# Gated linear attention followed by a bilinear feed-forward: natural feature order, prefix sums in two exact one-pass parts, v cast by the DMA, loads held behind the transposes, and a relaid program

## The chip, the cores and the metric

One core of one Trainium2 chip. The metric is the device time of one execution in microseconds (us). The kernel before was tuned already: 224.56 us, median of 3 runs (224.02 to 224.88). A profile is one traced execution; its span is about 2 us shorter than the time of the same run (222.4 against 224.5).

PE is TensorE (PEld its weight loads), DVE is VectorE, ACT is ScalarE, POOL is GpSimd, SP is SyncE. L207 is line 207 of that kernel's own file, so one piece of code has different line numbers in different kernels.

## The reference, cut to what matters

```python
# q, k, v, alpha: (4 batches, 8 heads, 768 steps, 48); 3072 tokens, d_model 384, d_ff 1536
for t in range(S):
    state = alpha[:, :, t, :, None] * state + einsum('bhd,bhe->bhde', k[:, :, t], v[:, :, t])
    y[:, :, t] = einsum('bhd,bhde->bhe', q[:, :, t], state)
x = y.transpose(0, 2, 1, 3).reshape(3072, 384)      # the 8 heads' 48 features side by side
out = ((x @ w_a) * (x @ w_b)) @ w_out
```

Both kernels work on six chunks: two batches (the chunk's two "units") times 256 steps each. For a chunk, a prefix sum of log alpha gives the decays; keys and queries scaled by them are transposed; scores, a masked product ("inner") and the product with the state brought along ("carried") make `y`; and `y`, evicted to SBUF as `xT`, feeds the two feed-forward matrices. The feed-forward of one chunk covers the attention of the next.

## The kernel before

The parts that the change touches:

```python
def stA(ch, u):                                  # prefix sum: one fp32 matmul
    nc.tensor.matmul(p, lhsT=ut_f32, rhs=ch.l2[:, u]..., start=True, stop=True)
...
def stS(ch, u):                                  # carried state
    for p in range(P2):
        for g in range(2):
            for r in range(2):                   # two row tiles, one PSUM bank (g)
                nc.tensor.matmul(y[rs, g, p, :], lhsT=state, rhs=queriesT(ch, u, p, g, rs), ...)
...
def stG(ch, u, eng):                             # 16 features of each head pair's block of 64 + 64 rows
    for t in range(KT):                          # come from the fourth pair's block, evicted first:
        for g in range(2):                       # six "gap" matmuls per unit, then a second eviction
            nc.tensor.matmul(ch.y[u][:, g, t, :], lhsT=gap[:, t]..., rhs=ch.xT[:, KT, 2 * g + u, :], ...)
    evac(ch, u, 0, KT, eng)
```

The heads lie in blocks of 64 rows of which 48 are used. So that the feed-forward contracts over three full tiles of 128 rows, the fourth block is moved into the free rows of the other three by matmuls, and the weight rows are loaded in that odd order (`load_ab`, 24 DMAs). All loads are fp32; chunk 2's keys and queries are transposed on TensorE, those of chunks 3 to 5 by a DMA transpose; loads go out as soon as their buffers are free. The order of work is a table (`START`, `PLAN`) of operations attached to feed-forward steps, and PSUM banks come from a rotating pool.

Of the kernel before, what the change touches and what calls it, by code (L numbers as in the profile page):

```python
# [9 lines left out]
BF16 = mybir.dt.bfloat16  # L10
AF = mybir.ActivationFunctionType
# [3 lines left out]
START = [  # L15
    (0, "new"), (0, "ln"), (0, "ld a 0 Y"), (0, "ld a 1 Y"), (0, "ld k 0 Y"), (0, "L 0 V"), (0, "ld q 0 Y"), (0, "warm 18"), (0, "ld v 0 Y"),
    (0, "ld k 1 Y"), (0, "ld q 1 Y"), (1, "new"), (0, "ld v 1 Y"), (0, "L 1 P"), (0, "A 0"), (0, "gate_w q 1"), (0, "W 0 512"), (0, "W 512 1024"),
    (1, "ld a * P"), (0, "W 1024 1536"), (0, "Wo 4 8"), (0, "Wo 0 4"), (0, "A 1"), (1, "ld v 0 P"), (0, "Wo 8 12"), (1, "ld k 0 P"),
    (1, "ld q 0 P"), (1, "ld q 1 P"), (0, "warm 24"), (1, "ld k 1 P"), (1, "ld v 1 P"), (0, "mk 0 V"), (0, "dec P"), (0, "v 0 S"), (0, "mq 0 V"),
    (0, "C 0 0 V"), (0, "warm 6"), (0, "C 0 1 S"), (0, "D 0 0 s2"), (0, "K 0 P y2"), (0, "warm 8"), (0, "warm 14"), (0, "v 1 S"), (0, "S 0"),  # L20
    (0, "mk 1 V"), (0, "D 0 1 s2"), (0, "mq 1 V"), (0, "warm 18"), (0, "Y 0 V"), (0, "C 1 0 V"), (0, "G 0 V"), (0, "D 1 0 s2"), (0, "C 1 1 S"),
    (0, "K 1 V y2"), (0, "ff 1 0"), (0, "ff 0 0"), (0, "S 1"), (0, "D 1 1 s2"), (0, "Y 1 S"), (0, "ff 3 0"), (0, "G 1 S"), (0, "ff 2 0"),
    (0, "ff 1 1"), (0, "ff 2 1"), (0, "ff 0 1"), (0, "ff 3 1"),
]



PLAN = {
    0: [(9, 1, "L * V"), (14, 1, "A 1"), (16, 1, "A 0"), (16, 1, "dec P"), (16, 2, "new"), (16, 2, "ld a * P"), (22, 2, "ld v * P"),
        (24, 1, "v 0 S"), (25, 1, "mk 0 V"), (25, 2, "ld k * P"), (25, 2, "ld q * P"), (25, 1, "mq 0 V"), (25, 1, "C 0 0 V"), (25, 1, "C 0 1 S"),  # L30
        (25, 1, "D 0 0 s2"), (25, 1, "K 0 P y2"), (26, 1, "mk 1 V"), (26, 1, "S 0"), (26, 1, "mq 1 V"), (26, 1, "D 0 1 s2"), (27, 1, "Y 0 S"),
        (27, 1, "v 1 S"), (27, 1, "C 1 0 V"), (27, 1, "C 1 1 V"), (27, 1, "G 0 S"), (27, 1, "D 1 0 s2"), (27, 1, "K 1 V y2"), (27, 1, "S 1"),
        (27, 1, "D 1 1 s2"), (27, 1, "ff 1 0"), (27, 1, "ff 3 0"), (27, 1, "Y 1 S"), (27, 1, "G 1 S"), (27, 1, "ff 0 0"), (27, 1, "ff 2 0")],
    1: [(0, 1, "ff 1 1"), (2, 3, "new"), (5, 1, "ff 3 1"), (5, 3, "ld k * P"), (5, 3, "ld a * P"), (6, 1, "ff 2 1"), (6, 2, "L * V"),
        (7, 3, "ld q * P"), (10, 1, "ff 0 1"), (10, 2, "A 0"), (10, 2, "A 1"), (11, 2, "mk 0 V"), (12, 2, "dec P"), (12, 3, "ld v * P"),
        (12, 2, "mq 0 V"), (13, 2, "mk 1 V"), (13, 2, "mq 1 V"), (14, 2, "C 0 0 V"), (14, 2, "v * S"), (15, 2, "C 0 1 S"), (15, 2, "C 1 0 V"),
        (15, 3, "L * P"), (16, 2, "D 0 0 s2"), (16, 2, "K * P"), (17, 2, "C 1 1 S"), (18, 2, "S 0"), (18, 4, "new"), (18, 2, "D 0 1 s2"),
        (19, 4, "ld q * P"), (19, 4, "ld k * P"), (20, 2, "D 1 0 s2"), (20, 2, "Y 0 S"), (20, 3, "A 0"), (20, 4, "ld v * P"), (21, 2, "G 0 V"),
        (21, 3, "mk 0 V"), (22, 3, "A 1"), (22, 2, "S 1"), (22, 2, "D 1 1 s2"), (23, 3, "mk 1 V"), (24, 2, "Y 1 S"), (25, 2, "G 1 S"),
        (25, 3, "mq 0 V"), (25, 3, "T 0 Y"), (26, 3, "mq 1 V"), (27, 3, "dec D"), (27, 3, "T 1 Y"), (27, 4, "ld a * P")],  # L40
    2: [(6, 3, "v * P"), (6, 3, "D 0 0 s2"), (8, 4, "L * P"), (9, 3, "K * V"), (10, 3, "S 0"), (10, 3, "D 0 1 s2"), (12, 5, "new"), (12, 3, "Y 0 S"),
        (13, 3, "D 1 0 s2"), (13, 3, "G 0 S"), (14, 4, "A 1"), (15, 3, "S 1"), (15, 3, "D 1 1 s2"), (16, 4, "A 0"), (16, 3, "Y 1 S"),
        (16, 4, "mk 0 V"), (19, 4, "mq 0 V"), (19, 4, "T 0 Y"), (20, 3, "G 1 S"), (22, 4, "mk 1 V"), (23, 4, "mq 1 V"), (24, 4, "v * S"),
        (24, 4, "dec D")],
    3: [(0, 4, "K * V"), (5, 5, "ld a * P"), (6, 5, "ld q * P"), (6, 4, "S 0"), (6, 4, "D 0 0 s2"), (7, 5, "ld v * P"), (7, 4, "D 0 1 s2"),
        (7, 5, "L * V"), (8, 4, "T 1 Y"), (9, 5, "ld k * P"), (11, 4, "D 1 0 s2"), (11, 4, "Y 0 S"), (12, 4, "G 0 S"), (12, 5, "A 0"),
        (13, 4, "S 1"), (13, 4, "D 1 1 s2"), (14, 5, "mk 0 V"), (14, 5, "A 1"), (15, 5, "mq 0 V"), (16, 4, "Y 1 V"), (16, 5, "dec D"),
        (19, 5, "mk 1 V"), (19, 4, "G 1 S"), (20, 5, "mq 1 V"), (20, 5, "T 1 Y"), (20, 5, "T 0 Y"), (26, 5, "v * V")],
    4: [(0, 5, "K * V"), (1, 5, "D 0 0 s2"), (6, 5, "D 1 0 s2"), (6, 5, "S 0"), (9, 5, "D 0 1 s2"), (12, 5, "Y 0 V"), (13, 5, "G 0 V"),
        (14, 5, "S 1"), (14, 5, "D 1 1 s2"), (17, 5, "Y 1 S"), (23, 5, "G 1 S")],  # L50
    5: [],
}
# [3 lines left out]
def kernel(  # L56
# [23 lines left out]
    G = DP - D  # L80
    HC = C // 2
    NT = B * C

# [5 lines left out]
    ps = ctx.enter_context(tc.tile_pool(name="ps", bufs=1, space=bass.MemoryType.PSUM))  # L89


    one = cst.tile([C, 1], F32, name="one")
    nc.vector.memset(one, 1.0)
    ident = cst.tile([C, C], BF16, name="ident")
    make_identity(nc, ident)

    ut_f32 = cst.tile([C, C], F32, name="ut_f32")
    make_upper_triangular(nc, ut_f32, val=1.0, diag=True)
    nc.vector.memset(ut_f32[0:HC, HC:C], 0.0)

    mask = cst.tile([C, 2, 2, HC], BF16, name="mask")
    mtmp = cst.tile([C, 2, 2, HC], BF16, name="mtmp")
    for t, first in ((mask, 0), (mtmp, -HC)):
        nc.gpsimd.memset(t, 0.0)
        nc.gpsimd.affine_select(out=t, in_=t, compare_op=ALU.is_gt, fill=1.0, base=first,
                                pattern=[[0, 2], [0, 2], [-1, HC]], channel_multiplier=1)
        nc.gpsimd.memset(t[:, 1, 0, :], 0.0)
        nc.gpsimd.affine_select(out=t[:, 1, 0, :], in_=t[:, 1, 0, :], compare_op=ALU.is_gt, fill=1.0, base=first + 1,
                                pattern=[[-1, HC]], channel_multiplier=1)

# [3 lines left out]

    S0 = [cst.tile([C, B, P2, DP], BF16, name=f"S0{i}") for i in range(2)]
    Sm = [cst.tile([C, 2, P2, DP], BF16, name=f"Sm{i}") for i in range(2)]
    Qp, Kp, QKp, bls = [], [], [], []
    for i in range(2):
        t = cst.tile([C, 2, 2, 2, H, DP], BF16, name=f"QKp{i}")
        (nc.gpsimd if i else nc.vector).memset(t[:, :, :, :, :, D:].rearrange("p b j r h d -> p (b j r h) d"), 0.0)  # L120
        QKp.append(t)
        Qp.append(t[:, :, 0])
        Kp.append(t[:, :, 1])
        t = cst.tile([C, B, P2], F32, name=f"bl{i}")
        (nc.gpsimd if i else nc.vector).memset(t, 0.0)
        bls.append(t)

    gap = cst.tile([C, KT, 2, DP], BF16, name="gap")
    nc.vector.memset(gap, 0.0)
    for t in range(KT):  # L130
        nc.vector.tensor_copy(gap[:, t, :, D:], ident.rearrange("p (r d) -> p r d", r=2)[:, :, t * G:(t + 1) * G])
    for i in range(2):
        for t in (S0[i], Sm[i]):
            (nc.gpsimd if i else nc.vector).memset(t, 0.0)
    nc.vector.tensor_copy(mask[HC:C], mtmp[HC:C])

    wa_t = cst.tile([128, KT, d_ff], BF16, name="wa_t")
    wb_t = cst.tile([128, KT, d_ff], BF16, name="wb_t")
    wo_t = cst.tile([128, NFF, d_model], BF16, name="wo_t")

    def load_ab(lo, hi):
        fs = slice(lo, hi)
        for w, t in ((moe_w_a, wa_t), (moe_w_b, wb_t)):
            two = w[:KT * 2 * D, fs].rearrange("(t r d) f -> r d t f", r=2, d=D)
            rest = w[KT * 2 * D:, fs].rearrange("(r t g) f -> r g t f", r=2, g=G)
            for r in range(2):
                nc.gpsimd.dma_start(out=t[r * DP:r * DP + D, :, fs], in_=two[r])
                nc.gpsimd.dma_start(out=t[r * DP + D:(r + 1) * DP, :, fs], in_=rest[r])

    def load_o(lo, hi):  # L150
        nc.gpsimd.dma_start(out=wo_t[:, lo:hi, :], in_=moe_w_out[lo * 128:hi * 128, :].rearrange("(k p) f -> p k f", p=128))



    class Chunk:
        def __init__(ch, c):
            ch.c = c
            ch.s, ch.b0 = c // 2, c % 2 * 2
            ch.kqT, ch.m, ch.y = {}, {}, {}

    chunks = [Chunk(c) for c in range(NCH)]
    ALL = slice(0, 2)
    ONE = (slice(0, 1), slice(1, 2))

# [321 lines left out]
```

## Time and profile before

| | before |
|---|---|
| span of the profile | 222.4 us |
| TensorE busy | 199.5 us (90%) |
| TensorE busy in 0-20, 20-40, 40-120, 120-218 us | 14.5, 17.9, 71.5, 95.6 us |
| warm-up matmuls | 88, 7.7 us |
| gap matmuls | 72, 6.0 us |

The prediction below shows the page. Here is the table of stretches in the four pieces that the accounting uses. The columns are the bounds, the length, busy time of PE, PEld, DVE, ACT and POOL, the granted clock, the DMA share and GB/s:

```profile
0.00:20.00 20.00, 14.47 (x290) 11.93 (x291) 13.03 (x24) 9.20 (x16) 13.14 (x34) 1.00 1.01 191
20.00:40.00 20.00, 17.94 (x281) 12.20 (x282) 12.80 (x23) 11.52 (x23) 16.16 (x24) 1.00 1.08 188
40.00:120.00 80.00, 71.48 (x1061) 43.36 (x1069) 55.54 (x75) 41.72 (x80) 26.44 (x23) 0.98 0.82 201
120.00:218.00 98.00, 95.58 (x931) 51.04 (x945) 50.64 (x69) 43.08 (x78) 0.00 (x0) 1.00 0.34 68
```

The length less the second figure is TensorE's idle time: 5.5, 2.1, 8.5 and 2.4 us. The clock of 0.98 in the third row is one spell at half clock, from 59.7 to 63.1 us.

In the list of waits a row has the engine, its line, what released it, then us in total, times, and the longest:

```profile
PE f L207 <- DVE l L187: 3.6, 1, 3.6
PE y L292 <- DVE Sm L343: 2.1, 1, 2.1
PE y L308 <- DVE m L282: 1.6, 2, 1.4
```

The first wait is the start; the others are attention that was hurried through with no feed-forward left to cover it. No DMA is in the list, though the DMA row is full for the first 72 us.

### The profile page before, as it was taken

Reading aid. Unit: us, or ns where it says so; the run is one execution under the profiler, and the core shown is the slowest. Engines: PE = TensorE matmul, PEld = TensorE weight load, DVE = VectorE, ACT = ScalarE, POOL = GpSimd, SP = SyncE. Lnnn points to the kernel's source line nnn. Section 1 sums busy time; section 2 is a strip of 40 time slices with the busy share of each in tenths; the row PEclk is TensorE's granted clock in tenths of the full one; section 3 lists DMA queues with packets and bytes.
Section 4 is the critical chain, followed back from the end, with each engine's and each line's share of the span. In section 5 each row is a group of like instructions: output and inputs, shape, how many; then the busy total and the mean of one; then the engine's idle time right before and its main releaser. Section 6 shows DMA issues by size and latency. Waiting matters only on the chain.

```text
span 222.4 us, 6004 instructions
## 1 busy us (share of the span) xinstructions
PE 199.5 (90%) x2558; PEld 118.5 (53%) x2584; DVE 132.0 (59%) x189; ACT 105.9 (48%) x195; POOL 55.7 (25%) x79
## 2 busy tenths in 40 slices
PE   3798799999799969899779999899999989999991
PEld 3487665566575545464345565464555445544460
DVE  5569657458736879942887914889508763045400
ACT  3470467742346955644517654577233334254420
POOL 8358949737200048400280000000000000000000
PEclk9999999999889999999999999999999999999997
DMA  7999999999999103999879945400881000320022
GB/s 168 261 175 154 200 181 168 271 266 323 325 282 259 38 3 82 265 271 180 65 173 264 197 114 113 93 0 4 126 172 37 3 3 0 83 58 3 0 71 71
DMA packets 37874, 30.70 MB, mean 138 GB/s; under 512 B 27084, under 2 KB 34008, under 8 KB 37848
## 3 DMA queue, kind: packets, MB, share of 16 engines
q0 software_dynamic: 8480, 19.27, 37.4%
q1 hardware_dynamic: 29368, 11.05, 25.6%
q8 instruction: 20, 0.33, 0.6%
q14 instruction: 6, 0.05, 0.1%
HBM read 25.97 MB, written 4.74 MB: 138 GB/s over the span
## 4 chain that ended last, share of the span: by engine, by line
PE 75%; DVE 12%; ACT 4%; issue 3%; DMA 2%; POOL 1%; SPq 1%; POOLq 0%; DVEq 0%; ACTq 0%
PE f L379 20%; PE f L360 19%; PE f L370 18%; PE f L207 4%; DVE m L282 4%; PE y L308 3%; PE s L281 3%; PE y L292 2%; PE f L254 1%; PE y L315 1%; DVE xT L297 1%; DVE kqT L260 1%; PE f L203 1%; DMA bl<-row 1%; DVE tmp L342 1%
## 5 line engine op out<-in xcount | busy, mean ns | idle before, releaser
L360 PE MATMUL f<-xT,wa_t 128*128 128x512 bf16 (+1 forms) x229 | 59.6, 361 | 1.2 <-ACT kqT L258 0.3
L370 PE MATMUL f<-xT,wb_t 128*128 128x512 bf16 (+1 forms) x225 | 59.0, 361 | 1.1 <-issue 0.5
L379 PE MATMUL f<-wo_t,prod 128*128 128x384 bf16 x288 | 48.6, 326 | 0.7 <-DVE prod L372 0.7
L379 PEld LDWEIGHTS <-prod 128*128 128x128 bf16 x288 | 27.8, 98 | 19.7 <-DVE prod L372 1.1
L360 PEld LDWEIGHTS <-wa_t 128*128 128x128 bf16 x240 | 22.5, 99 | 21.2 <-issue 1.0
L370 PEld LDWEIGHTS <-wb_t 128*128 128x128 bf16 x240 | 22.4, 99 | 21.2 <-issue 1.3
L282 DVE TENSOR_TENSOR m<-s,mask 128x1024 bf16<-128x1024 f32 x24 | 29.3, 1222 | 4.3 <-PE s L281 4.0
L381 ACT ACTIVATE ot<-f 128x384 f32<-128x384 f32 x24 | 11.8, 490 | 35.0 <-PE f L379 34.9
L187 POOL TENSOR_TENSOR l<-la 128x768 f32<-128x768 f32 (+1 forms) x3 | 4.6, 1532 | 41.1 <-ACT la L185 22.3
L299 ACT ACTIVATE xT<-y 128x256 bf16<-128x256 f32 (+1 forms) x18 | 10.7, 596 | 8.6 <-PE y L308 5.6
L207 PE MATMUL f<-l,ut_f 128*128 128x384 f32 x24 | 11.1, 562 | 3.6 <-DVE l L187 3.6
L215 DVE TENSOR_TENSOR QKp<-k_t,invb 128x768 bf16<-128x768 f32 x12 | 12.4, 1036 | 1.0 <-ACT invb L211 1.0
L281 PE MATMUL s<-kqT 64*64 64x128 bf16 x384 | 11.5, 222 | 1.4 <-DVE kqT L260 0.7
L215 DVE TENSOR_TENSOR QKp<-q_t,beta 128x768 bf16<-128x768 f32 x12 | 11.6, 977 | 0.5 <-DMA q_t<-in_q_dram 0.5
L342 DVE TENSOR_TENSOR tmp<-s,S 128x384 f32<-128x384 f32 x4 | 2.2, 558 | 15.5 <-PE s L329 15.5
L281 PEld LDWEIGHTS <-kqT 64*64 64x64 bf16 x384 | 7.7, 106 | 6.0 <-issue 3.9
L210 ACT ACTIVATE invb<-f 128x384 f32<-128x384 f32 x12 | 5.9, 492 | 10.0 <-DVE le L208 10.0
L185 ACT ACTIVATE la<-a_t 128x1536 f32<-128x1536 f32 (+1 forms) x7 | 9.1, 1295 | 3.1 <-DMA a_t<-in_alpha_dram 3.1
L208 DVE TENSOR_TENSOR le<-f,la 128x384 f32<-128x384 f32 x12 | 6.7, 556 | 4.9 <-PE f L207 4.7
L258 ACT ACTIVATE kqT<-f 128x1024 bf16<-128x1024 bf16 x5 | 5.1, 1022 | 9.0 <-PE f L254 8.9
L292 PE MATMUL y<-kqT,S 64*64 64x128 bf16 x96 | 7.0, 221 | 2.4 <-DVE tmp L342 1.5
L308 PE MATMUL y<-m,vx 64*48 64x128 bf16 x384 | 7.7, 220 | 1.6 <-DVE m L282 1.6
(233 smaller groups left out, 280.7 us busy)
## 6 DMA issues: line engine op xcount, KB each, us to landing
out_dram<-ot SPq DMA_DIRECT2D x48, 96.0 KB, 2.2
a_t<-in_alpha_dram POOLq DMA_DIRECT2D x5, 768.0 KB, 12.5
v_t<-in_v_dram POOLq DMA_DIRECT2D x4, 768.0 KB, 13.6
k_t<-in_k_dram POOLq DMA_DIRECT2D x4, 768.0 KB, 14.0
q_t<-in_q_dram POOLq DMA_DIRECT2D x4, 768.0 KB, 13.5
wo_t<-in_moe_w_out_dram POOLq DMA_DIRECT2D x3, 384.0 KB, 6.7
wa_t<-in_moe_w_a_dram POOLq DMA_DIRECT2D x6, 144.0 KB, 4.2
wb_t<-in_moe_w_b_dram POOLq DMA_DIRECT2D x6, 144.0 KB, 4.4
```

The source lines that it names most:

```text
L185: nc.scalar.activation(out=ch.la[:, us].rearrange("p b h r d -> p (b h r d)"), in_=ch.a[:, us].rearrange("p b h r d -> p (b h r d)"), func ...
L207: nc.tensor.matmul(p, lhsT=ut_f32, rhs=ch.l2[:, u].rearrange("p h d -> p (h d)"), start=True, stop=True)
L215: eng.tensor_mul(dst[ch.c % 2][:, u, :, :, :D], src[:, u].rearrange("p h r d -> p r h d"), by[:, u])
L281: nc.tensor.matmul(s2[g * HC:(g + 1) * HC, r, p, rk, :], lhsT=keysT(ch, u, 2 * h + p, g, r, rk), rhs=queriesT(ch, u, 2 * h + p, g, rs), st ...
L282: nc.vector.tensor_mul(m.rearrange("p r a k s -> p (r a) (k s)"), s2.rearrange("p r a k s -> p (r a) (k s)"), maskn(4))
L292: nc.tensor.matmul(y[rs, g, p, :], lhsT=lhsT, rhs=queriesT(ch, u, p, g, rs), start=(p == 0), stop=False, skip_group_check=True)
L299: nc.scalar.activation(out=o_, in_=i_, func=AF.Copy)
L308: nc.tensor.matmul(ch.y[u][r * DP:r * DP + D, g, p, :], lhsT=ch.vx[g * HC:(g + 1) * HC, u, 2 * p + r, rk, :], rhs=ch.m[u, p // 2][g * HC:( ...
L360: nc.tensor.matmul(ap, lhsT=wa_t[:, kk, f * 128:(f + 1) * 128], rhs=ff_x(ch, us)[:, kk], start=(kk == 0), stop=(kk == KT - 1))
L370: nc.tensor.matmul(bp, lhsT=wb_t[:, kk, f * 128:(f + 1) * 128], rhs=ff_x(ch, us)[:, kk], start=(kk == 0), stop=(kk == KT - 1))
L379: nc.tensor.matmul(op, lhsT=ch.prod[:, f, m * C:(m + 1) * C], rhs=wo_t[:, f, :], start=(f == 0), stop=(f == NFF - 1))
L381: nc.scalar.activation(out=ot, in_=op, func=AF.Copy)
```

## The change

Intent: lay `y` out in the natural order of the 384 features, so that the gap matmuls, the second eviction and the odd weight order go; replace each fp32 prefix sum by two float32r matmuls, one of the rounded values and one of the remainders; let the DMA cast v to bf16; order the carried-state matmuls so that neighbouring row tiles go to different banks; transpose chunk 2 by DMA as well; hold the next chunk's loads behind the transposes; and write the schedule as one program of single operations with explicit banks. The diff, cut to its core:

```diff
-def stA(ch, u): ... matmul(p, lhsT=ut_f32, rhs=ch.l2[:, u])
+def high(ch, us, eng): ... lh = float32r copy of l2                 # chunks 1 to 5
+def low(ch, us, eng):  ... ll = l2 - lh
+def cum2(ch, u, i):
+    for t in (ch.lh, ch.ll):
+        nc.tensor.matmul(p, lhsT=utr, rhs=t[:, u]..., start=(t is ch.lh), stop=(t is ch.ll))
...
-def stG(ch, u, eng): ... six gap matmuls, second eviction
+PIECES = [(h, j) for h in range(H) for j in range(D * h // DP, (D * h + D - 1) // DP + 1)]
+def inner(ch, u):          # 12 pieces of 64 rows, in natural order: 48 matmuls a unit (were 32)
+    ...
+def carried(ch, u, cross): # the two row tiles r in turn, with g = 1 - r: different banks
+    for n in range(3):
+        for c in range(2):
+            for r in range(2):
+                g = 1 - r if cross else r
+                if g == 0 and ch.s == 0: continue
+                ...
...
-            setattr(ch, n, ld.tile([C, 2, H, 2, D], F32, name=n + "_t"))
+            setattr(ch, what, ld.tile([C, 2, H, 2, D], BF16 if what == "v" else F32, name=what + "_t"))
...
+def gate_t(x, u):          # POOL touches the transposed tile: its queue waits for the transpose
+    nc.gpsimd.tensor_copy(go, x.kqT[int(u)][0:1, 0, 0, 0, 0:1])
...
-START = [...]; PLAN = {...}
+PROGRAM = """
+0: c1; warm 70 0; cz 0 V; cs 0 V
+...
+0: W b 768 1536; Ce 0 1 S; mq 1 V; warm 11 1
+...
+0: k 1 1 V; as 1 0; Y 1; SA 1; b 1 0 5; X 1 S; pr 1 0; as 0 0
+...
+2: v 0 S; gatet 1; D 1 0 2
+3: ld a * P
+...
+"""
```

In the program, `a`, `b`, `as`, `pr` and `o` are the feed-forward's matmuls, copy, product and output; `Y` is inner, `SA`/`SB` carried, `X` the eviction, `W` and `ld` loads, `warm n` n warm-up matmuls of 128 columns.

## The prediction

> **What bounds the kernel now.** I read the page's busy shares first, then the slices, then the table of stretches, then the chain that ended last piece by piece, to get the price of each piece of TensorE work.
>
> ```profile
> span 222.4 us, 6004 instructions
> PE 199.5 (90%) x2558; PEld 118.5 (53%) x2584; DVE 132.0 (59%) x189; ACT 105.9 (48%) x195; POOL 55.7 (25%) x79
> PE   3798799999799969899779999899999989999991
> DMA  7999999999999103999879945400881000320022
> ...
> PE 75%; DVE 12%; ACT 4%; issue 3%; DMA 2%; POOL 1%; SPq 1%; POOLq 0%; DVEq 0%; ACTq 0%
> ```
>
> TensorE is busy 90% and is 75% of the chain, so it is the bound. The DMA row is also full for the first 13 slices (72 us): a second limit early, which at present stops TensorE almost nowhere. Where TensorE is not full, the table of stretches says (a row has its bounds, its length, then PE, PEld, DVE, ACT and POOL busy, the granted clock, DMA share and GB/s):
>
> ```profile
> 0.00:10.00 10.00, 5.09 (x25) 3.40 (x26) 5.07 (x13) 3.71 (x5) 6.67 (x21) 1.00 0.98 210
> 20.00:30.00 10.00, 8.04 (x173) 6.61 (x172) 6.90 (x13) 4.13 (x9) 7.88 (x13) 1.00 1.07 198
> 50.00:60.00 10.00, 8.38 (x190) 5.87 (x187) 8.02 (x12) 2.90 (x5) 5.65 (x5) 0.98 1.05 324
> 110.00:120.00 10.00, 7.48 (x134) 4.43 (x137) 8.33 (x10) 4.08 (x9) 6.19 (x5) 1.00 1.06 204
> 200.00:210.00 10.00, 9.95 (x47) 4.54 (x47) 5.30 (x8) 4.74 (x8) 0.00 (x0) 1.00 0.01 2
> ```
>
> The last row is the pure feed-forward end, with nothing to wait for; the others are the start and the two worst stretches of attention. TensorE's idle of 22.9 us (222.4 - 199.5) splits, row by row of that table, into about 5.5 before 20 us, 2.1 from 20 to 40, 8.5 from 40 to 120, 2.3 from 120 to 218 and 4.4 behind the last matmul. The prices, from the chain:
>
> ```profile
> 38.51 0.83 PE s L236 x64
> ...
> 126.38 7.80 PE f L379 x48
> 134.83 0.66 PE s L329 x55
> ...
> 143.42 0.65 PE f L360 x3
> ...
> 146.26 0.34 PE y L315 x6
> ...
> 147.95 0.45 PE y L292 x12
> ...
> 149.49 0.65 PE f L207 x2
> ...
> 151.43 0.56 PE y L308 x32
> 151.99 0.75 PE f L370 x3
> ```
>
> A triple of 512-column feed-forward matmuls costs 0.65, an output matmul of 384 columns 7.80/48 = 0.1625. One fp32 prefix sum (384 columns) also costs 0.65. The carried-state group costs 0.45 for 16 (a few lie among the scores), 28 ns each; inner products 0.45 for 32, 14 ns each, plus 0.1 for coming from full-array work; the next full-array triple pays another 0.1 (0.75 for 0.65). State products cost 0.66/55 = 12 ns each, decay sums 0.83 a chunk, the gap-filling matmuls 0.34 a unit, eight transposes 0.45.
>
> **What the Trainium skill says.** "FP8 and Floating Point Precision", section TensorE Precision Notes: true FP32 makes four passes through the array. The trace agrees: 0.65 is 4.0 times 0.1625 at the same 384 columns. It does not price the float32r type in passes; no run here has it yet. "TensorE: Matmul & The Clock Gate", section "Wait — 56ns, not 53.3ns?": a warm matmul starts N/2.4 GHz plus about 2.5 ns after its predecessor; 384 columns give 162.5 ns, which the trace shows exactly. "TensorEngine Tiling (Array Packing)", sections Key Properties and Gotcha 1: changing the tiling mode drains the engine, and different row tiles can't use one PSUM bank at the same time. The trace has the drain (0.1 each way), and its carried-state group, which sends neighbouring row tiles to one bank, runs at 28 ns against 14 for scores. "DMA: Bandwidth & Descriptors", section Issuing engines are not separate DMA queues: all issuers share the same 16 engines. The trace agrees: SyncE's loads alone moved 261 GB/s from 4.5 to 13.6 us at a full DMA row, so early loads on both queues compete.
>
> **The change part by part** (TensorE microseconds, counts from the two instruction orders).
> - Prefix sums: chunks 1 to 5 replace 10 fp32 sums by two passes each. 10 x (0.65 - 2 x 0.1625) = -3.2. It adds a rounding copy (ACT 0.5 to 0.85) and a subtraction (DVE 0.95 for 768 columns, 0.56 for 384) per chunk: about 4 on ACT, 5 on DVE, before the sum, in engines at 48% and 59%.
> - Natural feature order: the 72 gap matmuls go, 12 x 0.34 = -4.1. Also gone is the two-step eviction (0.38 to 0.42, gap matmuls, 0.81), now one of about 0.81: some 0.7 less latency per unit, but only where TensorE has nothing else. It costs pieces that straddle a tile: inner products 384 to 576, +192 x 14 ns = +2.7.
> - Carried state: 192 to 240 matmuls (chunks 0 and 1 skip the zero state), ordered so that the two row tiles use different banks: 192 x 28 = 5.4 to 240 x 14 = 3.4, so -2.0.
> - Chunk 2 transposes and its decay go from TensorE to DMA: 32 transposes, -1.8, and 64 decay matmuls in the trace, -0.8. Last-state products are not made for the last two chunks: 384 to 320, -0.8.
> - Passages between tiling modes: 78 to 68, at 0.1, -1.0.
> - Feed-forward: the same columns. More half-width pairs (36 where there were 16), and the before trace shows 0.33 for a half triple against 0.65, so no TensorE cost; each extra ACT or DVE half pair costs some 0.15 of fixed time.
> The sum: -3.2 - 4.1 + 2.7 - 2.0 - 2.6 - 0.8 - 1.0 = -11.0. Priced this way the old kernel has 188.5 of TensorE work (feed-forward 140.1, attention 40.6, passages 7.8), the rest being 22.9 idle, about 7.5 of warm-up matmuls and some 3.5 of cold clock and latency. The new one has 177.5.
>
> Waits. Of the 8.5 idle between 40 and 120 us, most lies where a chunk's attention was hurried through while no feed-forward was left to cover it (the chain passes through evictions and exponentials from 71 to 79 us, and through the decay's DMAs at 105 to 110 us). The new program spreads scores, masks and outputs singly among feed-forward groups, with explicit banks and half-width groups of chunk 1. I credit half of these 8.5 and some of the later 2.3: -5.
>
> The start. Key and query of the first half come before the second half's decay input, and constants are fewer, so the first half's chain should be 1 to 2 earlier. Against that stand weights: the third weight block (columns 256 to 768 of the first matrix) is queued behind v, the first weight blocks and half of chunk 1. Reads up to and with it are 6 x 0.39 + 0.39 + 0.79 + 0.39 + 1.57 + 0.79 = 6.3 MB; at the 261 GB/s of SyncE's loads from 2 us on it lands at 26 us, while the first full block of feed-forward wants it at about 21. The old kernel had matmuls of that stage only from 22.4 on and reached continuous feed-forward at 28.6. So the start is about even; I charge +1.5. The wider weight DMAs (6 in place of 24) should avoid the hole seen in DMA from 14 to 18 us (103 GB/s).
>
> Casting v on the DMA saves little: the reads are the same, ACT and DVE still copy it into the padded layout. Loads behind transposes mean less contention for the latter; that is part of the waits above. The end (4.4 behind the last matmul) is unchanged.
>
> Total: 222.4 - 11.0 - 5 + 1.5 = 208 in the profile; the timed median is 2.1 over the profiled span, so 210; because the whole program was laid out for TensorE I shade it to 209.
>
> **The rivals.**
> - Weights or loads starve TensorE. For: the DMA row is full until 72 us and the old order had its weights earlier. Against: the old kernel's list of TensorE waits names no DMA at all. It would take back 3 to 8: 212 to 217.
> - float32r does not run in one pass. At two passes each, the 3.2 vanish and ACT and DVE work is added for nothing: about 213. At four, 10 x 0.65 is added on top: near 219.
> - The waits move. In-order engines now carry a fixed interleaving; a mask product on DVE (1.22 each, 24 of them) or an activation copy queued behind another chunk's exponentials holds a bank, and TensorE waits for it. For: explicit banks remove the pool's rotation, DVE stays near 132 to 137 busy. Against: 59% busy leaves room. Then only the 11 of TensorE work is won, or less: 213 to 216.
> - It goes better: most idle between 20 and 218 us (12.9) is covered. Then 222.4 - 11 - 9 = 202, timed 204.
>
> **Range and chances.** The -11.0 is counted and I trust it to 3 either way; waits and start are worth -10 to +4 between them. That gives 202 to 217. Slower by over 2% needs starvation beyond all the gains; within 2% means above 220.1, where two rivals must meet. Faster 0.90, same 0.07, slower 0.03.
>
> **What would show it.** Right: prefix matmuls of 384 columns spaced 0.16 apart; no gap matmuls; carried-state groups of 12 in about 0.17 plus passage; inner groups of 48 in 0.67; idle TensorE from 40 to 120 us near 4 and PE busy near 190 of 207. Wrong: waits of feed-forward matmuls on a weight DMA between 21 and 40 us; prefix matmuls at 0.33 or more; carried-state groups still at 28 ns each; TensorE idle of more than 10 after 40 us, released by mask products or activation copies.

## The result, and the profile after

209.97 us, median of 4 runs (209.25 to 210.48), against 224.72 (224.02 to 225.68) for the kernel before on the same chip. The ratio is 0.9339, 95% interval 0.9294 to 0.9384. A ratio here is the mean time of one kernel's fast runs over that of the other's fast runs of the same rounds, so it isn't quite the ratio of the medians. Executions over 1.5% slower than the fastest of the same kernel are left out of the means.

The page after:

```profile
span 207.3 us, 6249 instructions
PE 192.6 (93%) x2702; PEld 121.6 (59%) x2718; DVE 139.9 (67%) x223; ACT 101.2 (49%) x192; POOL 38.0 (18%) x54
PE   8988499999999989999998899999999999999991
...
PEclk9999859999999999999999999999999999999998
DMA  6999999999310697997959919699457200004155
...
PE 53%; issue 24%; DMA 9%; DVE 6%; ACT 4%; POOL 2%; POOLq 0%; ACTq 0%; DVEq 0%
```

TensorE is the bound as before, and fuller. (The 24% of "issue" in the chain are nearly all one piece of 39.5 us, from 36.6 to 76.2 us, in which the chain follows POOL as it waits at the first gate. TensorE was busy for 38.7 of these us.) Two things are new: the 4 in its fifth slice, and the 8 and 5 in the clock row at that place and just after it. The stretches say how much:

```profile
0.00:20.00 20.00, 17.34 (x351) 15.15 (x351) 16.17 (x30) 10.17 (x17) 14.82 (x30) 1.00 1.19 222
20.00:40.00 20.00, 16.67 (x236) 12.10 (x238) 10.29 (x22) 9.88 (x23) 8.90 (x9) 0.83 1.26 222
40.00:120.00 80.00, 76.52 (x1265) 50.52 (x1269) 63.26 (x101) 44.73 (x90) 9.54 (x10) 1.00 0.82 157
120.00:204.00 84.00, 82.04 (x853) 43.80 (x862) 50.20 (x71) 36.38 (x64) 4.76 (x5) 1.00 0.46 91
```

Idle from 40 to 120 us fell from 8.5 to 3.5 us, and behind 120 from 2.4 to about 1 (the last matmul ends near 203). But from 20 to 40 us TensorE idles 3.3 us where it was 2.1, and its mean clock there is 0.83.

The pieces of the chain (start, us, what) carry the new prices, and one DMA wait:

```profile
104.13 7.59 DMA a_t<-in_alpha_dram
...
116.36 0.34 PE psum L596 x2
...
137.51 0.17 PE psum L738 x12
```

The two one-pass matmuls of one prefix sum of 384 columns cost 0.34 us (the fp32 one cost 0.65 before), and twelve carried-state matmuls cost 0.17 us, 14 ns each (28 before).

TensorE's own waits after:

```profile
PE psum L738 <- issue: 2.5, 1, 2.5
PE psum L722 <- DVE prod L802: 1.7, 1, 1.7
...
PE psum L722 <- DMA kqT<-QKp: 0.6, 1, 0.6
```

"issue" means that TensorE waited for nothing that the profile shows. That longest wait is in TensorE's timeline (start, length, engine, line, operation, shape, count, and in brackets the idle time ahead):

```profile
22.27 0.81 PE L789 MATMUL psum<-xT,wa_t 128*128 128x256 bf16 x6 [0.64 <-ACT xT L773]
23.01 0.58 PE L738 MATMUL psum<-m,vx 64*64 64x128 bf16 x25
26.07 0.85 PE L738 MATMUL psum<-m,vx 64*64 64x128 bf16 x23 [2.48 <-issue]
```

The stall falls in the middle of 48 identical inner products of one unit, all on the same operands: 25 run, nothing for 2.48 us, then the other 23. At 24.8 us, during the stall, the clock drops to 0.50 and stays there until 31.6. TensorE is busy 5.6 us of these 6.8, of which half is lost: about 2.8.

So the 15.1 us of the span (222.4 - 207.3) come from: TensorE work -11.0 (as priced; tested below), waits from 40 us on -6.4 (5.0 + 1.4), the spell at half clock of the kernel before, which is gone, -1.7; what remains, +4, is the start. Read directly the start gives a little more: warm-up matmuls 11.2 us for 7.7 (+3.5), half clock +2.8, idle before 40 us 6.0 for 7.6 (-1.6), +4.7 in all. The two readings differ by 0.7, which is the accuracy of this account. (The warm-ups fill time in which TensorE would have waited, so what they and the smaller idle time come to is best read together.)

### The profile page after: what moved, and what is told of

The parts are those of the page before. It is cut to its first block, busy times and chain, and to the rows that moved or that the text cites. A ratio compares the mean times of both kernels' runs of the same rounds, so it can differ in the third digit from the quotient of the medians.

```text
span 207.3 us, 6249 instructions
## 1 busy us (share of the span) xinstructions
PE 192.6 (93%) x2702; PEld 121.6 (59%) x2718; DVE 139.9 (67%) x223; ACT 101.2 (49%) x192; POOL 38.0 (18%) x54
## 2 busy tenths in 40 slices
DMA packets 52587, 29.42 MB, mean 142 GB/s; under 512 B 42760, under 2 KB 49672, under 8 KB 52560
## 4 chain that ended last, share of the span: by engine, by line
PE 53%; issue 24%; DMA 9%; DVE 6%; ACT 4%; POOL 2%; POOLq 0%; ACTq 0%; DVEq 0%
PE psum L789 28%; PE psum L812 15%; DMA a_t<-in_alpha_dram 7%; PE psum L738 4%; DMA kqT<-QKp 2%; ACT la L553 1%; DVE l L559 1%; PE psum L722 1%; PE psum L693 1%; ACT kqT L660 1%; PE psum L574 1%; PE psum L596 1%; DVE S L518 1%; DVE vx L513 1%; DVE m L727 1%
## 5 line engine op out<-in xcount | busy, mean ns | idle before, releaser
L789 PE MATMUL psum<-xT,wa_t 128*128 128x512 bf16 (+1 forms) x262 | 57.2, 344 | 1.3 <-ACT xT L773 0.6
L789 PE MATMUL psum<-xT,wb_t 128*128 128x512 bf16 (+1 forms) x262 | 56.4, 338 | 0.6 <-issue 0.5
L812 PE MATMUL psum<-wo_t,prod 128*128 128x384 bf16 x288 | 51.5, 326 | 0.1
L727 DVE TENSOR_TENSOR m<-psum,mask 128x1024 bf16<-128x1024 f32 x24 | 29.0, 1220 | 7.9 <-PE psum L722 7.7
L773 ACT ACTIVATE xT<-psum 128x768 bf16<-128x768 f32 x11 | 8.9, 808 | 14.4 <-PE psum L738 14.3
L553 ACT ACTIVATE la<-a_t 128x768 f32<-128x768 f32 (+1 forms) x8 | 9.3, 1165 | 11.6 <-DMA a_t<-in_alpha_dram 11.6
L738 PE MATMUL psum<-m,vx 64*64 64x128 bf16 x576 | 10.9, 221 | 2.8 <-issue 2.5
L722 PE MATMUL psum<-kqT 64*64 64x128 bf16 x384 | 10.3, 219 | 2.7 <-DVE prod L802 1.7
L570 PE MATMUL psum<-wz 128*128 128x128 bf16 x154 | 11.2, 238 | 1.0 <-DVE one L493 1.0
L570 PEld LDWEIGHTS <-wz 128*128 128x128 bf16 x154 | 10.3, 108 | 1.9 <-DVE one L493 1.0
```

What stands on the lines that cost most here:

```text
L553: nc.scalar.activation(out=ch.la[:, us].rearrange("p b h r d -> p (b h r d)"), in_=ch.a[:, us].rearrange("p b h r d -> p (b h r d)"), func ...
L570: nc.tensor.matmul(w[:, :C], lhsT=wz, rhs=wz, start=True, stop=True)
L722: nc.tensor.matmul(s2[g * HC:(g + 1) * HC, r, p, rk, :], lhsT=ch.kqT[u][rs, 1, rk, 2 * h + p, g * HC:(g + 1) * HC], rhs=queriesT(ch, u, 2 ...
L727: nc.vector.tensor_mul(m.rearrange("p r a k s -> p (r a) (k s)"), ch.s2[u, h].rearrange("p r a k s -> p (r a) (k s)"), maskn(4))
L738: nc.tensor.matmul(y[c * DP:(c + 1) * DP, g, j // 2 * C:(j // 2 + 1) * C], lhsT=lhsT, rhs=rhs, start=(g, c) not in begun, stop=False, skip ...
L773: nc.scalar.activation(out=o_, in_=i_, func=AF.Copy)
```

## The experiments

Ten kernels, in three sets on two chips; the kernel before had medians of 225.25 us in the first set and 224.99 and 224.95 in the others. Two further ideas never ran. Putting the carried-state matmuls back into the order in which neighbouring row tiles write one bank was rejected by the race check, so the 14 ns against 28 stand as read from the traces alone. And loading v as fp32 does not fit beside the rest: the work pool then wants 96 KB a partition, and 92.5 are left.

The question is why the start cost +4. Before the runs I counted the matmuls and weight loads that TensorE had begun at each stall. In the kernel after, the two stalls on "issue" near 20 and 24 us lie ahead of counts 705 and 961, 256 apart. The page lists an instruction queue of 21 packets, 0.34 MB, so 16 KB each, and TensorE's 5,420 matmuls and weight loads are 21 times 256 and a few over. The Trainium skill, "Trainium Architecture — The Big Picture", section The software stack, gives an instruction 64 bytes; then a packet is 256 of them, which agrees with the distance of the stalls. That is the theory of the instruction fetch: TensorE runs dry because the next block comes late over DMA engines that are full of loads. The rival from the prediction is weights that come late.

### wide_warm: fewer instructions ahead of the stall

```diff
-    wz = cst.tile([C, C], BF16, name="wz")
+    wz = cst.tile([C, 512], BF16, name="wz")
-        for _ in range(n):
-            nc.tensor.matmul(w[:, :C], lhsT=wz, rhs=wz, start=True, stop=True)
+        for _ in range(-(-n // 4)):
+            nc.tensor.matmul(w[:, :512], lhsT=wz[:, :C], rhs=wz, start=True, stop=True)
```

> The warm-up matmuls are 512 columns wide, a quarter as many: the same TensorE time, some 220 TensorE instructions fewer in the first 20 us. Theory (the 2.48 us stall among the second unit's inner products is a late 16 KB fetch of TensorE's own instructions, and the half clock from 24.8 to 31.6 us follows from it): no stall over 1 us in that group, no half clock before 200 us, time 3 to 5 below the changed kernel (205 to 207), unless a weight wait of up to 1.5 shows in its place. Rival (the stall is a weight or mask wait that the profile misses): the stall stays in the same group and the time stays at 210.

206.81 us (205.46 to 207.73), ratio 0.9189 [0.9139, 0.9239]: 1.6% faster than the change. The time fell as expected, but neither of the two signs came: a stall of over 1 us remained, and so did a half clock. The stall, 1.88 us, fell after another number of the same inner products:

```profile
23.49 0.36 PE L738 MATMUL psum<-m,vx 64*64 64x128 bf16 x11
25.72 1.14 PE L738 MATMUL psum<-m,vx 64*64 64x128 bf16 x37 [1.88 <-issue]
```

Its stalls now lie ahead of counts 447 and 703: again 256 apart, though the work around them is other work. The half clock lasted 3.4 us in place of 6.8.

### more_warm: more instructions ahead of it

```diff
-0: c1; warm 70 0; cz 0 V; cs 0 V
+0: c1; warm 90 0; cz 0 V; cs 0 V
```

> 20 more warm-up matmuls (40 instructions) in the first batch, before anything depends on them. Fetch theory: the gaps are tied to the count of TensorE instructions, 256 apart, so the long gap moves 40 instructions up the program: it falls after about 5 of the 48 inner products of the second unit and no longer after 25, and the short one near 20.2 us moves by as many. Rival (a data wait): the gap stays after 25 inner products. Time within 1 per cent of the changed kernel.

Forty more instructions ahead (20 matmuls and their 20 weight loads), and the stall moves forty instructions back in the work, from the 25th to the 5th inner product. That is what a boundary in the instruction stream does; a late weight or operand would stop the same matmul as before.

```profile
24.98 0.30 PE L738 MATMUL psum<-m,vx 64*64 64x128 bf16 x5
27.36 0.81 PE L738 MATMUL psum<-m,vx 64*64 64x128 bf16 x43 [2.08 <-issue]
```

The stalls lie ahead of counts 705 and 961, as in the change; the first of them grew to 1.54 us.

206.69 us in one run (its state is unknown), 1.6% below the change, where I had expected it within 1%. The stall of 2.08 us was there, but there was no half clock from 24 to 34 us (1.00 throughout), and the run was 3 us faster than the change. So most of the cost of the start seems to hang on the clock that falls after the stall, rather than on the stall; it is one run.

### fp32_sums: the prefix sums undone

```diff
-        for t in (ch.lh, ch.ll):
-            nc.tensor.matmul(p, lhsT=utr, rhs=t[:, u]..., start=(t is ch.lh), stop=(t is ch.ll))
+        cum(ch, u, i)                                # one fp32 matmul, as in chunk 0
-        "H": lambda x, u, e: high(x, us(u), ENG[e]),
-        "L": lambda x, u, e: low(x, us(u), ENG[e]),
+        "H": lambda x, u, e: None,
+        "L": lambda x, u, e: None,
```

> All prefix sums in fp32 as before, the rounding copies and subtractions dropped. Theory of the prediction: TensorE gets 10 x 0.32 = 3.2 us of work back, so 2.5 to 3.5 slower than the changed kernel (212.5 to 213.5). Rival (two passes behind a copy and a subtraction save nothing, because the chain through ACT and DVE is longer): within 1 us of the changed kernel, or faster.

212.37 us (210.49 to 213.35), ratio 0.9431 [0.9372, 0.949]; against the change's 0.9339 that is 1.0%, some 2.1 us, a little under the 2.5 to 3.5 that I expected. In the profile the span is 210.8 (+3.5) and TensorE is busy 196.0 us (+3.4; predicted 3.2). One chain piece shows the old price back:

```profile
118.74 0.65 PE psum L574 x2
```

So float32r ran in one pass and the first term of the sum holds, even with what the rounding copies and subtractions cost ACT and DVE.

### no_gates: the loads let loose

```diff
-2: v 0 S; gatet 1; D 1 0 2
+2: v 0 S; D 1 0 2
-3: gatet 1
-4: gatet 1
```

> The three waits of the loads for the transposes are taken out; the loads start when their buffers are free. Theory (the gates put transpose, then load, on the chain: 7.1 per cent of it is the load of alpha, and TensorE stands 1.7 us near 113 us): 1 to 2 us faster, the 1.7 us wait gone. Rival (the gates protect the transposes): transposes land later than 4.3 us in the median, scores wait for them, 1 to 4 us slower.

219.18 us median (215.08 to 228.01). Only two of the six runs count as fast (217.98 and 215.08); their ratio is 0.9631 [0.9533, 0.973], 3.1% above the change: 6 to 7 us lost. My theory, that the gate only delays loads, fell. The rival was right in direction, and the effect was larger than it said; its sign was not quite: the median from issue to landing of the transposes stayed 4.3 us, and the longest rose from 4.4 to 8.4. The profiled run was one of the slow ones at 218.8, so I use it for the kind of wait and not for its size. From its list of TensorE's waits:

```profile
PE psum L720 <- DMA kqT<-QKp: 10.4, 4, 5.0
```

and from its chain:

```profile
72.25 11.48 DMA kqT<-QKp
...
100.30 17.48 DMA kqT<-QKp x2
```

TensorE waits 10.4 us for transposed tiles where it waited 0.6 with the gates, and behind two of these waits its clock falls to half (81.0 to 87.8 and 108.3 to 111.7 us). k, q and v were issued at 72.6 to 75.5 us, with the transposes in flight (issued at 70.3); with the gates the first load behind the transposes was issued at 76.9, after they had landed. All issuers share the 16 engines, as the prediction noted; this run shows what that costs a transfer that is urgent.

### after_again: the change once more, on the other chip

No edit.

> The changed kernel unaltered, for comparison on this chip: ratio to the kernel before 0.93 to 0.94, 209 to 211; the stall before TensorE instruction 961 again 2 to 2.5 us, followed by 3.4 or 6.8 us of half clock or by none, as the clock's window falls.

Runs of 209.66, 210.75, 209.56, 205.95, 211.87 and 211.4, median 210.2. The stall is there again, 2.48 us ahead of count 961, with half clock from 25.0 to 31.8. The one fast outlier had a mean clock of 0.995 where the others have 0.98, so it had hardly any half clock. Since every other run is over 1.5% above it, there is no ratio. The outlier is about 4 us faster than the rest. The trace puts the spell of half clock at 2.8 us, and one run without a trace can't say where the remainder lies.

### fp32_v32: the cast of v by itself

fp32_sums frees the room that `lh` and `ll` took, so v fits as fp32 there:

```diff
-ld.tile([C, 2, H, 2, D], BF16 if what == "v" else F32, name=what + "_t")
+ld.tile([C, 2, H, 2, D], F32, name=what + "_t")
```

> As the run with all sums in fp32, and v loaded as fp32 and not cast by the DMA (both copies of v do not fit beside the split sums' tiles, so it goes on top of that run). Theory of the prediction: the cast saves no reads and no copies, so the same as the run with fp32 sums within 1 us (ratio 0.94 to 0.95). Rival (casting DMAs of 192-byte rows are slow, or the fp32 source slows the copies): more than 1.5 us apart in either direction.

212.76 us (210.88 to 213.62), ratio 0.9453 [0.9399, 0.9508] against fp32_sums' 0.9431: the same. The DVE's copy of v rose from 353 to 554 ns and the DMA packets fell from 52,587 to 41,451, and neither mattered. What the cast gives is room in SBUF, without which the other parts don't fit.

### fill: feed-forward work across the boundary

```diff
-0: k 1 1 V; as 1 0; Y 1; SA 1; b 1 0 5; X 1 S; pr 1 0; as 0 0
-1: l2 0 V
-0: a 5 0 2
-1: H 0 S
-0: a 3 0 4; as 5 0; a 4 1 5
+0: k 1 1 V; as 1 0; as 0 0; b 1 0 5; a 5 0 2; a 3 0 4; Y 1; SA 1; b 0 0 1; X 1 S; pr 1 0
+1: l2 0 V; H 0 S
+0: as 5 0; a 4 1 5
```

(`b 0 0 1` is taken out of its old place.) Six feed-forward matmuls of 256 columns and their weight loads are 12 instructions and took 0.74 us (22.27 to 23.01 above); 12 instructions of inner products take 0.08. So moving such groups ahead gives the fetch time.

> Three half-width feed-forward groups that are ready, or nearly, go ahead of the second unit's inner products, so that they run while TensorE's next instruction block is fetched (18 instructions, 1 us of work), and one more behind them. Fetch theory: the stall before instruction 961 shrinks from 2.5 to 1 to 1.5 us, the block still arrives near 26 us; 1 us saved, and some 2 more if the half clock after it stays away: 206.5 to 209. A weight wait of up to 1 us may show ahead of the group on columns 640 to 768. Rival (the start is bound by the weights anyway): no gain, TensorE waits as long for a weight DMA.

207.72 us (206.42 to 208.91), ratio 0.9231 [0.9177, 0.9285], as expected. The stall shrank to 0.51 us, further than the 1 to 1.5 expected, and the clock was 1.00 from 20 to 120 us:

```profile
25.36 0.42 PE L736 MATMUL psum<-m,vx 64*64 64x128 bf16 x16
26.29 0.64 PE L736 MATMUL psum<-m,vx 64*64 64x128 bf16 x32 [0.51 <-issue]
```

A wait of 0.67 us for the weight columns from 256 on appeared, the first and only sign of the weights that the prediction feared.

### fill_w: the same with earlier weights

fill, with both loads of columns 256 to 768 moved ahead of chunk 1's v.

> As the one before, and the weight blocks of columns 256 to 768 are loaded before the v of chunk 1's first half, so they land some 2 us earlier. If weights bound the reordered start: another 0.5 to 1 us faster than the one before. Rival (instruction fetch alone sets the start): the same as it within 0.5 us.

207.94 us (206.47 to 211.08), ratio 0.9247 [0.918, 0.9313]: the same as fill. The wait for weights is gone, but the stall on issue is 1.63 us: the missing instructions come at 26.29 us in fill and at 26.28 here. So here the instructions set the start, not the weights.

### late_loads: the same instructions, with the DMA engines free

The decisive run, a diagnosis and not a candidate. All loads that the first 23 us don't need (weight columns from 256 on, half of chunk 1, chunk 2, the output matrix) go behind one gate on the last mask product of chunk 0:

```diff
-0: ...; W a 256 768; ...; W b 256 768; ...; W a 768 1536; ...
-0: W b 768 1536; ...     1: ld a 1 P ... ld v 1 P     2: ld a * P ... ld v * P     0: Wo 0 6; Wo 6 12
+0: ...; M 1 1; gatem; W a 256 768; W b 256 768; W a 768 1536; W b 768 1536
+1: ld a 1 P; ld k 1 P; ld q 1 P; ld v 1 P
+0: Wo 0 6; Wo 6 12
+2: ld a * P; ld k * P; ld q * P; ld v * P
+        "gatem": lambda x: nc.gpsimd.tensor_copy(go, x.m[1, 1][0:1, 0, 0, 0, 0:1]),
```

> A diagnosis, not a candidate: every load that the first 23 us do not need (all weight columns from 256 on, the second half of chunk 1, chunk 2, the output matrix) is issued only behind a gate on the last mask product of chunk 0, near 23 us. TensorE's instructions are the same ones in the same order as in the changed kernel. If the instruction fetch is slow because it shares 16 full DMA engines with the loads, the 16 KB packet that began at 23.75 and the resumption at 26.07 both come earlier by a microsecond or more, the long stall ahead of instruction 961 (2.48 us in the changed kernel) shrinks under 0.7 us, and no half clock follows at 24.8; TensorE then waits for weight columns 256 and up, 3 to 6 us near 25 to 32, so the profiled span rises to 208 to 213. If the fetch takes as long whatever the loads do, the stall ahead of instruction 961 stays near 2.5 us in the middle of the group of 48 inner products, although the DMA engines are nearly free at that time.

210.46 us in one run (state unknown), span 208.5. The DMA view from 22 to 24 us (the busy row in 40 slices of 0.05 us, then the packets and the instruction queue), first of the change, then of this run:

```profile
DMA  8998999999999799899999999998999999999979
...
DMA packets 421, 0.42 MB, mean 212 GB/s; under 512 B 25, under 2 KB 420, under 8 KB 420
...
q8 instruction: 1, 0.02, 3.0%
```

```profile
DMA  1000000000000900000000000000000000000000
...
DMA packets 7, 0.02 MB, mean 9 GB/s; under 512 B 6, under 2 KB 6, under 8 KB 6
...
q8 instruction: 1, 0.02, 2.9%
```

In the first the instruction packet is one of 421; in the second it stands nearly alone (the single 9). And TensorE's timeline there:

```profile
23.93 0.58 PE L733 MATMUL psum<-m,vx 64*64 64x128 bf16 x25
25.07 0.53 PE L733 MATMUL psum<-m,vx 64*64 64x128 bf16 x23 [0.56 <-issue]
...
29.53 1.22 PE L784 MATMUL psum<-xT,wa_t 128*128 128x256 bf16 x9 [3.34 <-DMA wa_t<-in_moe_w_a_dram]
```

The stall sits at exactly the same instruction, 25 inner products in, and is 0.56 us in place of 2.48 (2.48 also in after_again, fp32_sums and no_gates, and 2.76 in fp32_v32). The weights, issued late on purpose, then cost 3.34, as expected, and behind that wait the clock fell to half from 30.5 to 33.9 us.

This measures the fetch. In the change, TensorE crosses the boundary at count 705 at 20.15 us, the next packet begins at 23.75 (3.6 us later) and ends at 24.70, and TensorE resumes at 26.07: 5.9 us from one block to the next. Here it crosses at 21.06, the packet begins at 22.68 (1.6 later) and ends at 23.61, and TensorE resumes at 25.06: 4.0 us. So, by this one run, waiting behind the loads made 1.9 us of the stall of 2.48. The rest is a fetch that takes 4.0 us even on free engines, when TensorE needs only 3.4 us for these 256 instructions (20.15 to 23.59, and 21.06 to 24.50).

### fill_wide: both mendings

> Both mendings of the start in one kernel: feed-forward groups ahead of the second unit's inner products, and warm-up matmuls of 512 columns (228 fewer instructions). Alone they gave ratios of 0.9231 and 0.9189 against the kernel before. Theory: they attack the same loss (the fetch stall and the half clock behind it, about 4 us in all), so together they give little more than the better of the two: 205 to 207 us, ratio 0.913 to 0.920, and no half clock between 20 and 200 us. Rival: they add, 203 us or less. Second rival: with the wide warm-ups the stall falls on instruction 703, inside other work than the moved groups cover, and the time is that of the wide warm-ups alone with its short spell of half clock.

205.69 us (204.29 to 206.44), ratio 0.9131 [0.9081, 0.9182]. This is the best version: 2.2% faster than the change (0.9131 against 0.9339), 8.7% faster than before. The first theory was right, at the low end of its range: together they gain 0.6% over the wide warm-ups alone (intervals that overlap) and 1.1% over fill alone, so mostly they mend the same loss. The clock row of its page is full:

```profile
PEclk9999999999999999999999999999999999999999
```

and in TensorE's timeline the stalls that are left fall among the warm-ups and behind the second inner product:

```profile
20.86 0.82 PE L568 MATMUL psum<-wz 128*128 128x512 bf16 x3 [1.56 <-issue]
...
26.77 0.86 PE L736 MATMUL psum<-m,vx 64*64 64x128 bf16 x46 [0.68 <-issue]
```

## Why the prediction was right or wrong

The median (209.0 against 209.97) and the range were right. The sum was right in its largest term, and two of the others were off in opposite directions (waits 1.4 us better, the start 2.5 worse), so it is partly luck that the total came so close.

- **TensorE work, -11.0: right as a sum.** PE busy fell by 6.9 us; with 3.5 more of warm-ups and 1.1 more of half clock (2.8 against 1.7), work fell by 11.5. The term of the prefix sums is shown by an experiment (3.4 for 3.2). The gap matmuls are gone and a carried-state matmul takes 14 ns, as the trace shows. Inner products at 14 ns (46 between 20.36 and 21.00 us), chunk 2's transposes and the passages between tiling modes were not tested one by one: that each has its predicted share is read or argued, only the sum is checked. And the reason that the prediction gave for the 28 ns, two row tiles in one bank, is not what the trace before shows: there the two matmuls of a pair, which do write one bank (in different rows), start 3 to 4 ns apart, although the page that the prediction cites rules this out, and it is the next pair, in the other bank, that comes 53 ns later. By the code, every pair uses the same two of the array's four 64x64 tiles (row tile r, output rows r), while the new layout uses all four in turn; in the trace after, four matmuls start within some 10 ns, and the next four 56 ns after the first. That fits both traces, but no run tests it.
- **Waits, -5: too low by 1.4, and their parts are not separated.** They gave 6.4. I put the credit on the spreading of attention among feed-forward and called the loads behind the transposes "part of the waits". No run undid the spreading, so its share is not shown. Nor is the 6.4 the gates' doing: TensorE waited for no DMA in the kernel before, and the transposes there landed in 4.4 to 6.1 us without gates. What the gates do is keep the new program, with its 8 DMA transposes for 6, from losing 6 to 7 us (two fast runs; without them the ratio is 0.9631), and that the prediction did not price. It also placed the old idle badly: from 71 to 79 us TensorE idled 1.0 us and from 105 to 110 it idled 0.1, while the longest waits between 40 and 120 us lay at 58 and 80 us and, right behind the second stretch, from 110 to 112. What the gates cost is small: the chain waits 7.6 us for the next chunk's alpha from 104 us on, runs over its logarithm and sum to a product on DVE, and there makes TensorE wait the 1.7 us that the list shows at L802.
- **The start, +1.5: the step that failed.** The prediction charged it for weights ("the third weight block ... lands at 26 us, while the first full block of feed-forward wants it at about 21"). In the change no matmul of the first 40 us waits for a weight. The start lost about 4 us, to a stall of 2.48 us for TensorE's own instructions and to the half clock behind it. That the DMA row was full was seen; that the instructions travel over it was not in my reckoning. fill_wide, where the half clock is gone and the stalls are shorter, wins 2.2% back.
- **The cast of v: right**, worth nothing in time. **The tail: right**, 4.3 us for 4.4.
- **The rivals.** Weights that starve TensorE: only when the fetch was mended (0.67 us in fill), or on purpose. float32r in two or four passes: no. Moved waits: one of 1.7 us on a product. The better outcome (204) was near: fill_wide reached 205.69 once the start was mended.

What stays open: why a fetch takes 4.0 us when the packet itself takes 0.9. What starts it was not tested either, but in the ten kept traces with the early loads of the change the packet begins 3.5 to 3.8 us after TensorE crosses the boundary ahead of the long stall, whatever the work around it; so it is probably the crossing.

And why did the clock fall after the stall of 2.48 us but not after that of 2.08 in more_warm? The Trainium skill, "TensorE: Matmul & The Clock Gate", section What's actually happening, describes a free-running window of 3413 ns, so that it depends on where the window lies. The kept traces agree: every spell from one clock change to the next is a whole number of windows (20.48, 6.83 and 3.41 us are 6, 2 and 1). Laid on this grid, the stall of more_warm falls across the end of a window at 25.94 us, and the two windows have 1.3 and 1.4 us of idle TensorE; the shorter stall of wide_warm lies within one window (22.50 to 25.91), which has 2.1 us of idle. In all kept traces a window at full clock with 1.86 us or more of idle was followed by half clock, and one with less was not, but for one of 1.62 us in the kernel before (one of 1.66 us in no_gates was not). This is read from the traces: one run in six of the unchanged kernel kept its clock, and no run moved the window by itself.

## What to carry to other kernels

Count instructions as well as microseconds: where a tight stretch of small matmuls meets a full DMA row, the instructions themselves come late, so use few wide warm-up matmuls and put long matmuls between the short ones. A wait on "issue" in the middle of identical matmuls, at counts 256 apart and moved by adding instructions ahead, is the sign of it. And hold bulk loads back until an urgent DMA transpose has landed: here that was worth 6 to 7 us, more than any single saving of work on TensorE.

## What the Trainium skill lacked or had wrong

- "Trainium Architecture — The Big Picture", section The software stack, has the instruction streams moved to each engine at load. Here 21 instruction packets of 16 KB moved during the execution. Another page, "Runtime: NRT & Kernel Launch", section Instruction fetch mechanics, does describe this fetch in 16 KiB blocks of 256 instructions, which the counts 256 apart confirm, but calls the cost of crossing a block boundary mostly hidden: here a late block stopped TensorE for 2.48 us (0.56 with nearly free DMA engines). No page prices a late block.
- "TensorE: Matmul & The Clock Gate", section What's actually happening, gives the half clock after at least one idle window of 3.4 us. Here it began at 24.8 us, 1.2 us into the stall, and TensorE had been idle for 1.86 of the 3.41 us of the window that ended there (0.64 + 1.2): a partly idle window is enough.
- "FP8 and Floating Point Precision", section TensorE Precision Notes, has four passes for true FP32 (agreed: 0.65 us for 384 columns) but no price for float32r: 0.34 us for two matmuls of 384 columns, one pass each.
- "DMA: Bandwidth & Descriptors", section Rules for kernel authors, says that a transpose next to ordinary DMAs needs nothing. For correctness no run contradicts it; for time, TensorE waited 10.4 us for transposes that ran beside loads, and 0.6 when the loads were held back.
- "TensorEngine Tiling (Array Packing)", section Key Properties, has the drain at a change of mode without a figure: about 0.1 us each way, by the trace before.
